# Windowed attention into a softplus MLP: scores of the first three blocks as 64x64 fp32 matmuls, v products of the first two in 64 columns

## The chip, the cores and the metric

The kernel runs on one core of a Trainium2 chip. The metric is the device time of one execution in microseconds (us), taken as the median of several runs. A core has five engines that run side by side, each through its own queue in order: TensorE (PE, matmuls, with the weight loads shown apart as PEld), VectorE (DVE), ScalarE (ACT), GpSimd (POOL) and SyncE (SP), which here issues all DMAs.

## The reference

Eight batches of 576 tokens, eight heads of 64. Each token attends to itself and the 63 tokens before it; the result goes through a two-layer MLP with softplus between.

```python
batch, n_heads, seq, head_dim = (8, 8, 576, 64)
window = 64
scores = scale * np.matmul(q, k.transpose(0, 1, 3, 2))
mask = (rel >= 0) & (rel < window)
scores = np.where(mask, scores, -1000000000.0)
attn = np.exp(scores - np.max(scores, axis=-1, keepdims=True))
attn = attn / (np.sum(attn, axis=-1, keepdims=True) + 1e-09)
...                                  # x: 4608 tokens x 512
h = x @ w_in                         # 512 x 2048
g = np.maximum(h, 0.0) + np.log1p(np.exp(-np.abs(h)))
return (g @ w_out).astype(np.float32)   # 2048 x 512
```

The inputs are fp32 except the two weights, which come in float64 and are handed over as 64-bit words.

## The kernel before

The 4608 tokens are cut into 12 blocks of `TB` = 384. For each block the attention is done in four head pairs (`hp`), each of two heads that together fill 128 partitions; a pair yields 128 rows of the transposed x, kept as two fp32r parts (`x0_*`, `x1_*`). The MLP of a block is 16 steps f: `ffn_up` makes 128 rows of h in 12 matmuls (L405; four pairs by three products of the parts), ACT and DVE form softplus (L409 to L416: `u`, then two fp32r parts `g`), and `ffn_down` adds 9 matmuls (L426) into three PSUM banks. `ffn_up` has two PSUM buffers (`ps_h`), which the DVE's L413 frees.

The passes over f are: block 0 for f 0 to 7, block 1 for all 16, block 0 for f 8 to 15, and then one block after another. Before a step can run, its 1 MB of weights must be loaded and made fp32 from the words (`load_w`: ACT L170, DVE L171 to L174, ACT L177, POOL L178). For f 0 to 11 one set of instructions handles both weights (128x1024, tiles `raws` and `ws`); for f 12 to 15 there are two sets of half the width (128x512, `raw` and `wh`).

Attention comes in two forms. Blocks 0 and 1 (`by_pe`; the first two of `ORDER`, tokens from 0 and from 1152, each at the start of a batch; block 2 holds the tokens from 384) do it in plain fp32: one matmul of 384 columns for each tile of 128 queries gives both heads' scores, because k lies in a block-diagonal tile `kbd` with zeros in the other head's rows (L258). DVE's L269 scales the 192 key columns of a tile and head, adds the mask, keeps the minimum of the negated scores; L275 folds the last 64 columns onto the first 64; ACT takes exp (L279), DVE divides (L284 to L287), the PE transposes (L294), and the product with v takes 12 matmuls, each with a 128-column weight tile `v_pad` in which the other head's columns are zero (L351). All other blocks split q, k into fp32r parts on ACT and DVE (L240 to L247), use 12 matmuls for the scores of a pair (L262), transpose the probabilities by DMA (L311, L316) and multiply bf16 parts of p and v (L380).

The order is set in two ways. Stages of attention, weight conversions and MLP steps are events with a place on one axis (`BASE`, `PACE`, `STG`, `CONVERT`), and are written out in that order. Up to place 100 (some 50 steps) a scheduler that knows estimated durations then orders the instructions of each engine; from there on the PE's order is as written. Once built, every queue is fixed, and at run time each engine waits at its next instruction.

Of the kernel before, what the change touches and what calls it, by code (L numbers as in the profile page):

```python
# [8 lines left out]
F32 = mybir.dt.float32  # L9
BF16 = mybir.dt.bfloat16  # L10
# [21 lines left out]
PE_ORDERED_FROM = 100  # L32
MANUAL = {mybir.EngineType.PE}
# [5 lines left out]
def window_attention_softplus_ffn(  # L39
# [24 lines left out]
    nc = tc.nc  # L64
# [43 lines left out]
    W = CH + P  # L108
# [13 lines left out]
    v_pads = [att.tile([P, 2, NJ, 2, P], F32, name="v_pad", tag=n) for n in ("nat", "tr")]  # L122
    for t in v_pads:
        nc.vector.memset(t, 0.0)
# [4 lines left out]
    mask = cpool.tile([P, W], BF16, name="mask")  # L129
    nc.gpsimd.memset(mask, 0.0)  # L130
    nc.gpsimd.affine_select(
        out=mask, in_=mask, pattern=[[1, W]], compare_op=ALU.is_gt, fill=FAR, base=0, channel_multiplier=-1
    )
    nc.gpsimd.affine_select(
        out=mask, in_=mask, pattern=[[-1, W]], compare_op=ALU.is_ge, fill=FAR, base=CH, channel_multiplier=1
    )

    mask_c = cpool.tile([P, W], BF16, name="mask_c")
    nc.gpsimd.tensor_copy(mask_c, mask)
    nc.gpsimd.memset(mask_c[:, 0:CH], FAR)  # L140
# [43 lines left out]
    def attention(g, hp):  # L184
# [3 lines left out]
        by_pe = g < 2  # L188
# [11 lines left out]
        if by_pe:  # L200
            qf = ld.tile([P, 2, TB], F32, name="q_in") if hp % 2 else ld.tile([P, 2, W - P + TB], F32, name="k_in")
            qf = qf[:, 0, 0:TB]
            kf = kbd_s[hp % 2]
            skip = CH if t0 == 0 else 0
            nc.sync.dma_start(qf, qT[c0 : c0 + P, t0 : t0 + TB])
            for hh in range(2):
                nc.sync.dma_start(kf[heads[hh], hh, skip:], kT[c0 + hh * D : c0 + (hh + 1) * D, t0 - CH + skip : t0 + TB])
        else:
            q_in = ld.tile([P, 2, TB], F32, name="q_in")
            k_in = ld.tile([P, 2, W - P + TB], F32, name="k_in")  # L210
            ts, ks = slice(t0, t0 + TB), slice(t0 - CH, t0 + TB)
# [38 lines left out]
        st = att.tile([P, 2, NJ, W], F32, name="st", bufs=2)  # L250
        mn = att.tile([P, 2, NJ], F32, name="mn", bufs=2)
        sm = att.tile([P, 2 * NJ], F32, name="sm", bufs=2)
        for j in range(NJ):
            sp = bank()
            spv = sp[:, : 2 * W].rearrange("p (h c) -> p h c", h=2)
            js, kc = slice(j * P, (j + 1) * P), slice(j * P, j * P + W)
            if by_pe:
                mm(spv, qf[:, js], kf[:, :, kc], start=True, stop=True)  # L258
# [136 lines left out]
    part = {}  # L395
# [131 lines left out]
```

## Time and profile before

| | |
|---|---|
| median of 3 runs (lowest, highest) | 1041.5 us (1039.78, 1042.13) |
| span of the profiled execution | 1042.4 us |
| PE busy over the span | 990.4 us |
| DVE, ACT, POOL busy | 812.8, 740.3, 56.0 us |
| mean granted TensorE clock | 0.975 |

The profiled execution has no other time of its own than its span, which lies 0.9 us above the median of the runs. In the profile a matmul in plain fp32 is two records (L258, L351), one in fp32r or bf16 is one. A row of a group gives the line, the engine, the operation, output and input tiles, the shape and count, then busy us and mean ns of one, then idle time of the engine just before and what ended it. A row of stretches gives for each engine the busy us and the number of instructions in the stretch.

### The profile page before, as it was taken

The page shows a single profiled execution, that of the slowest core. Times are in us where ns is not written, and L with a number is a line of the kernel's source. Part 1 is how long each engine was busy: PE and PEld are TensorE (multiplying, and loading weights), DVE is VectorE, ACT ScalarE, POOL GpSimd, SP SyncE. Part 2 cuts the span into 40 slices and gives each one's busy share as a digit, 9 for nine tenths or more (in the row PEclk, how much of TensorE's full clock was granted, in tenths as well). Part 3 has the DMA queues.
Part 4 walks back from the last instruction along what each step waited for, and adds up shares of the span by engine and source line. Part 5 has one row for each costly group of instructions (what it writes and reads, how often), then busy time and mean ns, then how long its engine had stood idle before and what let it go on. Part 6 is the DMA issues. An engine that isn't in the chain of part 4 may idle for free.

```text
span 1042.4 us, 16725 instructions
## 1 busy us (share of the span) xinstructions
PE 990.4 (95%) x5888; PEld 879.7 (84%) x5888; DVE 812.8 (78%) x1797; ACT 740.3 (71%) x1705; POOL 56.0 (5%) x54
## 2 busy tenths in 40 slices
PE   5879589999989999999999999999999999999998
PEld 3667478888778889989989989989989998998997
DVE  6889989776977687987987987987987987875322
ACT  4575569777867677877877877877877877875443
POOL 3223520000000000000000000000000000000000
PEclk9889869999999999999999999999999999999999
DMA  6585246435463345744544544543543654731000
GB/s 200 142 274 176 85 146 159 99 97 126 128 146 82 89 104 99 148 108 97 146 113 99 146 111 96 145 114 93 148 115 87 154 114 90 148 53 31 31 1 31
DMA packets 209748, 119.06 MB, mean 114 GB/s; under 512 B 143360, under 2 KB 201728, under 8 KB 208128
## 3 DMA queue, kind: packets, MB, share of 16 engines
q1 hardware_dynamic: 209664, 118.00, 45.7%
q8 instruction: 46, 0.75, 0.3%
q14 instruction: 38, 0.31, 0.1%
HBM read 76.28 MB, written 10.22 MB: 83 GB/s over the span
## 4 chain that ended last, share of the span: by engine, by line
PE 71%; DVE 2%; DMA 1%; ACT 1%; issue 0%; SPq 0%; ACTq 0%; DVEq 0%
PE ps_h L405 31%; PE ps_o L426 31%; PE ps_a L380 4%; PE ps_a L262 4%; DMA tr<-nat 1%; DMA v_in<-in_v_dram 0%; DVE st L269 0%; DVE v L332 0%; DVE raw L443 0%; DVE u L413 0%; DVE nat L314 0%; DVE k L247 0%; ACT nat L310 0%; DVE g L416 0%; DVE xf L386 0%
## 5 line engine op out<-in xcount | busy, mean ns | idle before, releaser
L405 PE MATMUL ps_h<-x,w 128*128 128x384 f32 x2304 | 449.1, 342 | 9.4 <-DVE u L413 7.5
L426 PE MATMUL ps_o<-w,g 128*128 128x512 f32 x1728 | 435.0, 395 | 2.3 <-ACT g L415 2.1
L405 PEld LDWEIGHTS ps_h<-x,w 128*128 128x128 f32 x2304 | 407.1, 190 | 25.4 <-DVE u L413 10.1
L426 PEld LDWEIGHTS ps_o<-w,g 128*128 128x128 f32 x1728 | 317.8, 188 | 61.4 <-ACT g L415 3.0
L409 ACT ACTIVATE u<-ps_h 128x384 f32<-128x384 f32 x192 | 94.0, 489 | 129.5 <-PE ps_h L405 122.8
L413 DVE SCALAR_TENSOR_TENSOR u<-ps_h,u 128x384 f32<-128x384 f32 x192 | 106.3, 554 | 74.4 <-ACT u L411 73.2
L279 ACT ACTIVATE st<-st,mn 128x128 f32<-128x128 f32 x288 | 111.9, 390 | 15.7 <-DVE st L275 15.7
L416 DVE TENSOR_TENSOR g<-u,g 128x384 fp32r<-128x384 f32 x192 | 106.9, 558 | 11.9 <-ACT g L415 9.4
L269 DVE CUSTOM_DVE_ANT_0 st<-ps_a,mask 128x192 f32<-128x192 f32 x216 | 69.7, 352 | 49.4 <-PE ps_a L262 45.8
L410 ACT ACTIVATE u<-u 128x384 f32<-128x384 f32 x192 | 100.6, 525 | 3.3
L411 ACT ACTIVATE u<-u 128x384 f32<-128x384 f32 x192 | 100.3, 522 | 3.8
L262 PE MATMUL ps_a<-k,q_hl 128*128 128x192 f32 x480 | 77.3, 285 | 0.0
L380 PEld LDWEIGHTS <-v 128*128 128x128 bf16 x1088 | 56.1, 98 | 23.9 <-issue 22.1
L380 PE MATMUL ps_a<-tr,v 128*128 128x128 bf16 (+1 forms) x1088 | 70.1, 213 | 3.4 <-DMA tr<-nat 3.4
L415 ACT CAST g<-u 128x384 fp32r<-128x384 f32 x112 | 57.0, 509 | 21.9 <-DVE u L413 21.1
L262 PEld LDWEIGHTS ps_a<-k,q_hl 128*128 128x128 f32 x480 | 67.6, 195 | 3.4
L310 ACT CAST nat<-st 128x768 bf16<-128x768 f32 x40 | 33.2, 830 | 38.4 <-DVE st L308 38.3
L279 ACT ACTIVATION_READ_ACCUMULATOR st<-st,mn 128x1 f32 x288 | 54.0, 187 | 0.0
L385 ACT COPY xf<-ps_a 64x384 f32<-64x384 f32 x80 | 38.1, 477 | 21.2 <-PE ps_a L380 20.1
L287 DVE TENSOR_TENSOR st<-st,sm 128x768 f32<-128x768 f32 x48 | 50.0, 1041 | 1.2
L386 DVE TENSOR_TENSOR xf<-ps_a,xf 64x384 f32<-64x384 f32 x80 | 43.8, 548 | 5.8 <-ACT xf L385 4.6
L329 DVE TENSOR_TENSOR v_in<-v_in,v 128x896 f32<-128x896 f32 x40 | 43.5, 1087 | 4.3 <-ACT v L328 4.3
(82 smaller groups left out, 899.4 us busy)
## 6 DMA issues: line engine op xcount, KB each, us to landing
k_in<-in_kT_dram SPq DMA_DIRECT2D x80, 224.0 KB, 3.8
v_in<-in_v_dram SPq DMA_DIRECT2D x80, 224.0 KB, 3.7
q_in<-in_qT_dram SPq DMA_DIRECT2D x84, 192.0 KB, 4.1
raws<-in_w_words_dram SPq DMA_DIRECT2D x12, 1024.0 KB, 6.0
out_dram<-raw SPq DMA_DIRECT2D x12, 512.0 KB, 2.8
raw<-in_w_words_dram SPq DMA_DIRECT2D x8, 512.0 KB, 5.2
out_dram<-raw SPq DMA_DIRECT2D x12, 256.0 KB, 2.6
v_pad<-in_v_dram SPq DMA_DIRECT2D x52, 32.0 KB, 2.4
```

The lines of the kernel that those rows point to most:

```text
L262: mm(spv[:, hh, :], q_hl[:, hh, js], part[:, hh, kc], start=(hh == 0 and i == 0), stop=(hh == 1 and i == 1), skip_group_check=True,)
L269: nc.vector.tensor_tensor_reduce(st[:, hh, j, :], spv[:, hh, :], m, QSCALE, 3.0e38, ALU.add, ALU.min, mn[:, hh, j : j + 1])
L279: nc.scalar.activation(sv[:, i, 0:P], sv[:, i, 0:P], AF.Exp, bias=mn[:, hh, j : j + 1], scale=-1.0, accum_out=sm[:, i : i + 1])
L380: mm(av[:, osl], (v13 if s else v12)[:, c, hh, :, :], src, start=(i == 0), stop=(i == len(passes) - 1), skip_group_check=True,)
L405: mm(hv, weight(0, a, f)[:, c * P : (c + 1) * P], x[b][c], start=(i_mm == 0), stop=(i_mm == 3 * NC - 1))
L409: nc.scalar.activation(u, hv, AF.Abs)
L410: nc.scalar.activation(u, u, AF.Exp, scale=-1.0)
L411: nc.scalar.activation(u, u, AF.Ln, bias=1.0)
L413: nc.vector.scalar_tensor_tensor(gf, hv, 0.0, u, ALU.max, ALU.add)
L415: (nc.scalar.copy if g < 2 or f % 2 else nc.vector.tensor_copy)(gt[0], gf)
L416: nc.vector.tensor_tensor(gt[1], gf, gt[0].bitcast(F32), ALU.subtract)
L426: mm(ops[g][j], gt[a][:, js], weight(1, b, f), start=(first and i == 0), stop=(last and i == 2),)
```

## The change

For blocks 0, 1 and 2 (`quad`) the scores become 12 matmuls a pair, each of 64 contraction rows (one head), 64 queries and 128 keys; four of them, two heads by two halves of a query tile, use different quarters of the PE array. Each row of scores then holds 128 key columns, not 192: the reduction reads 128 columns and the fold (L275) is gone for these blocks. q and k stay as loaded (`q_two`, `k_two`, both with a half for even and a half for odd pairs), so block 2 has no fp32r split any more. Block 2's probabilities lie otherwise, and its product with v takes 40 matmuls a pair in place of 28. Blocks 0 and 1 hold v without zeros (`v_first`) and multiply 64 weight columns at a time, 12 matmuls a pair as before. New masks of 128 columns are made on POOL; the big memsets of `kbd` and `v_pad` go.

```diff
-    kbd_s = [att.tile([P, 2, CH + TB], F32, name="kbd", tag=f"k{i}") for i in range(2)]
...
+    q_two = ld.tile([P, 2, TB], F32, name="q_two", tag="q_in")
+    k_two = ld.tile([P, 2, CH + TB], F32, name="k_two", tag="k_in")
+    nc.gpsimd.memset(k_two[:, :, 0:CH], 0.0)
...
-    v_pads = [att.tile([P, 2, NJ, 2, P], F32, name="v_pad", tag=n) for n in ("nat", "tr")]
-    for t in v_pads:
-        nc.vector.memset(t, 0.0)
+    v_first = [att.tile([P, 2, NJ, P], F32, name="v_first", tag=n) for n in ("nat", "tr")]
+    for t in v_first:
+        nc.vector.memset(t[0:CH, 0, 0, :], 0.0)
...
+    mask_q = att.tile([P, 3, P], BF16, name="mask_q", tag="k0")
...
-        by_pe = g < 2
+        by_pe = g < BY_PE        # 2
+        quad = g < QUADS         # 3
...
-            nc.sync.dma_start(qf, qT[c0 : c0 + P, t0 : t0 + TB])
-            for hh in range(2):
-                nc.sync.dma_start(kf[heads[hh], hh, skip:], kT[c0 + hh * D : c0 + (hh + 1) * D, t0 - CH + skip : t0 + TB])
+            nc.sync.dma_start(qf, qT[c0 : c0 + P, ts])
+            nc.sync.dma_start(kf[:, skip:], kT[c0 : c0 + P, t0 - CH + skip : t0 + TB])
...
-                for j in range(j0, NJ):
-                    dst = v_pad[rows, lay, j, :, :].rearrange("p h (i d) -> p (h i) d", i=2)[:, 0:4:3, :]
-                    s = start + j * P
-                    nc.sync.dma_start(dst, v[s : s + n, c0 : c0 + P].rearrange("p (h d) -> p h d", h=2))
+                rows_of_v = v[start + j0 * P : start + NJ * P, c0 : c0 + P]
+                nc.sync.dma_start(vf[rows, lay, j0:, :], rows_of_v.rearrange("(j p) n -> p j n", p=P)[0:n])
...
+        if quad:
+            sp = [bank()[:, :TB].rearrange("p (j c) -> p j c", j=NJ) for hh in range(2)]
+            for j in range(NJ):
+                for b, half in enumerate(heads):
+                    for hh, rows in enumerate(heads):
+                        at = j * P + b * CH
+                        mm(
+                            sp[hh][half, j, :], qf[rows, at : at + CH], kf[rows, at : at + P],
+                            start=(j == 0), stop=(j == NJ - 1), skip_group_check=True,
+                        )
+            for j in range(NJ):
+                for hh in range(2):
+                    scaled_min(hh, j, sp[hh][:, j, :])
+                yield
...
-            if by_pe:
-                mm(spv, qf[:, js], kf[:, :, kc], start=True, stop=True)
...
-        nc.vector.tensor_tensor(sv[:, :, 0:CH], sv[:, :, 0:CH], sv[:, :, P:], ALU.min)
+        if not quad:
+            nc.vector.tensor_tensor(sv[:, :, 0:CH], sv[:, :, 0:CH], sv[:, :, P:], ALU.min)
...
-                    mm(
-                        av[:, cs], v_pad[:, a % 2, a // 2, hh, :], pt[:, hh, cs],
-                        start=(hh == 0 and a == 0), stop=(hh == 1 and a == 2 * NJ - 1), skip_group_check=True,
-                    )
+                        for h2, cols in enumerate(heads):
+                            mm(
+                                av[cols, cs], vf[:, a % 2, a // 2, cols], pt[:, h2, cs],
+                                start=(a == 0), stop=(a == 2 * NJ - 1), skip_group_check=True,
+                            )
...
+                        for f in (1, 0):
+                            a = c - f
+                            if 0 <= a < 2 * NJ:
+                                at = ((s * 2 + hh) * 2 * NJ + a // 2 * 2 + f) * P + a % 2 * CH
+                                if f == 1 and c % 2 == 0 and c < NCH - 1:
+                                    passes.append((s, c, trf[:, at : at + P], slice(a * CH, a * CH + P)))
+                                    break
+                                passes.append((s, c, trf[:, at : at + CH], slice(a * CH, a * CH + CH)))
+                        continue
```

Since the scheduler's estimates change, the order of everything up to place 100 changes too. Names such as `x_3_1` below are the x of pair 3 of block 1; line numbers of the changed kernel run 4 to 30 higher (L258 there is the reduction, L268 the scores, L369 the v products, L435 the up matmuls, L443 the `u` step).

At the end of block 1's attention the DVE's order was (L357 the x of its last pair, L241 the split of block 2's q, L171 to L173 a half weight conversion):

```order
L173 SCALAR_TENSOR_TENSOR wh<-raw,wh 128x512
L174 SCALAR_TENSOR_TENSOR wh<-raw,wh 128x512
L357 TENSOR_TENSOR x_3_1_891<-ps_a,x_3_1_890 128x384
L241 TENSOR_TENSOR q_hl<-q_in,q_hl 64x768
L171 TENSOR_SCALAR wh<-wh 128x512
L172 TENSOR_SCALAR wh<-wh 128x512
L173 SCALAR_TENSOR_TENSOR wh<-raw,wh 128x512
```

Now twelve reductions of two pairs of block 2 follow that x, and then these rows up to the first `u` step (L300 to L303 the division, L175 to L177 a half conversion, L443 the `u` step):

```order
L300 TENSOR_SCALAR sm<-sm 128x6
L301 RECIPROCAL sm<-sm 128x6
L303 TENSOR_TENSOR st<-st,sm 128x6x128
L175 TENSOR_SCALAR wh<-wh 128x512
L176 TENSOR_SCALAR wh<-wh 128x512
L300 TENSOR_SCALAR sm<-sm 128x6
L177 SCALAR_TENSOR_TENSOR wh<-raw,wh 128x512
L301 RECIPROCAL sm<-sm 128x6
L443 SCALAR_TENSOR_TENSOR u<-ps_h,u 128x384
```

So between x_3_1 and the first `u` step of block 1 the DVE has twelve reductions, two row sums, one division and three rows of a half conversion, where before it had four reductions, the q split and five rows of half conversions.

On the PE the same place read before (L351 the last v product, L262 the scores of block 2's first pair, of which there are twelve rows):

```order
L351 MATMUL ps_a<-pt,v_pad 128x64 x12
L405 MATMUL ps_h<-x_3_1_890,w_85 128x384 x2
L405 MATMUL ps_h<-x_3_1_891,w_85 128x384
L405 MATMUL ps_h<-x_3_1_890,w_86 128x384
L405 MATMUL ps_h<-x_3_1_891,w_85 128x384
L405 MATMUL ps_h<-x_3_1_890,w_86 128x384
L262 MATMUL ps_a<-k_1145,q_hl 128x192
```

and reads now:

```order
L268 MATMUL ps_a<-k_two,q_two 64x128 x2
L369 MATMUL ps_a<-pt,v_first 64x64 x11
L268 MATMUL ps_a<-k_two,q_two 64x128 x10
L435 MATMUL ps_h<-x_3_1_880,w_85 128x384 x2
L435 MATMUL ps_h<-x_3_1_881,w_85 128x384
L435 MATMUL ps_h<-x_3_1_880,w_86 128x384
L435 MATMUL ps_h<-x_3_1_881,w_85 128x384
L435 MATMUL ps_h<-x_3_1_880,w_86 128x384
L268 MATMUL ps_a<-k_two,q_two 64x128 x24
```

The scores of three pairs of block 2 stand here, where one pair's stood.

More of the change, by code (lines that the diff above doesn't have):

```diff
@@ L32 @@
 PE_ORDERED_FROM = 100
+BY_PE, QUADS = 2, 3
 MANUAL = {mybir.EngineType.PE}
@@ L136, in window_attention_softplus_ffn @@
     )
-    mask_c = cpool.tile([P, W], BF16, name="mask_c")
-    nc.gpsimd.tensor_copy(mask_c, mask)
-    nc.gpsimd.memset(mask_c[:, 0:CH], FAR)
+    mask_q = att.tile([P, 3, P], BF16, name="mask_q", tag="k0")
+    mask, mask_c, mask_b = [mask_q[:, i, :] for i in range(3)]
+    for m in (mask_c, mask, mask_b):
+        nc.gpsimd.tensor_copy(m[0:CH, :], wide[0:CH, 0:P])
+        nc.gpsimd.tensor_copy(m[CH:P, :], wide[CH:P, CH:W])
+    nc.gpsimd.memset(mask_c[0:CH, 0:CH], FAR)
+    nc.gpsimd.memset(mask_b[CH:P, 0:CH], FAR)
@@ L248, in attention @@
         yield
[L250 removed]
+        width = P if quad else W
+        st = att.tile([P, 2, NJ, W], F32, name="st", bufs=2)[:, :, :, 0:width]
         mn = att.tile([P, 2, NJ], F32, name="mn", bufs=2)
         sm = att.tile([P, 2 * NJ], F32, name="sm", bufs=2)
[L253 to L271 removed]
@@ new lines, in attention @@
+        for j in range(NJ if not quad else 0):
+            spv = bank()[:, : 2 * W].rearrange("p (h c) -> p h c", h=2)
+            js, kc = slice(j * P, (j + 1) * P), slice(j * P, j * P + W)
+            for hh in range(2):
+                for i, part in enumerate((k_hi, k_lo)):
+                    mm(
+                        spv[:, hh, :], q_hl[:, hh, js], part[:, hh, kc],
+                        start=(hh == 0 and i == 0), stop=(hh == 1 and i == 1), skip_group_check=True,
+                    )
+            for hh in range(2):
+                scaled_min(hh, j, spv[:, hh, :])
@@ L348, in attention @@
             if by_pe:
[L349 to L355 removed]
+                if hh == 0:
+                    for a in range(2 * NJ):
+                        cs = slice(a * CH, (a + 1) * CH)
+                        for h2, cols in enumerate(heads):
+                            mm(
+                                av[cols, cs], vf[:, a % 2, a // 2, cols], pt[:, h2, cs],
+                                start=(a == 0), stop=(a == 2 * NJ - 1), skip_group_check=True,
+                            )
+                else:
                     nc.scalar.copy(x_t[0], av[:, :TB])
```

61 lines of the change are left out of this document (24 added, 37 removed).

## The prediction

> **What bounds the kernel now.** I read the page's slices first, then a table of stretches, then the end of the prologue in order of time.
>
> ```profile
> span 1042.4 us, 16725 instructions
> ...
> PE   5879589999989999999999999999999999999998
> ...
> DVE  6889989776977687987987987987987987875322
> ...
> PEclk9889869999999999999999999999999999999999
> ```
>
> The PE is nearly full from the sixth slice on (a slice is 26 us), and shows holes only before. The stretches put numbers to that (per engine: busy us and instructions; then granted clock, DMA share, GB/s):
>
> ```profile
> core 0: us, PE busy (x) PEld busy (x) DVE busy (x) ACT busy (x) POOL busy (x), PEclk, DMA share, GB/s
> 0.00:138.00 138.00, 99.78 (x475) 80.51 (x476) 117.02 (x233) 75.10 (x193) 49.86 (x50) 0.87 0.56 173
> 0.00:20.00 20.00, 9.13 (x17) 4.84 (x18) 12.12 (x35) 7.16 (x18) 8.74 (x24) 1.00 0.65 181
> 20.00:60.00 40.00, 34.79 (x181) 28.60 (x180) 31.43 (x80) 21.70 (x69) 8.28 (x6) 0.83 0.64 194
> 60.00:120.00 60.00, 48.79 (x250) 40.48 (x249) 58.83 (x100) 37.39 (x85) 24.59 (x15) 0.94 0.54 177
> 120.00:146.00 26.00, 11.97 (x49) 11.15 (x50) 20.43 (x38) 14.30 (x35) 10.25 (x8) 0.55 0.44 141
> 146.00:300.00 154.00, 148.79 (x901) 131.65 (x900) 124.66 (x279) 119.48 (x280) 4.15 (x3) 0.98 0.49 121
> 300.00:1042.40 742.40, 736.99 (x4496) 663.00 (x4495) 565.29 (x1271) 540.28 (x1224) 0.00 (x0) 1.00 0.43 101
> ```
>
> Three regimes. Behind 146 us the PE is the limit (148.8 of 154, 737 of 742.4): there only PE work counts. From 60 to 120 us the DVE is the limit (58.8 of 60). From 120 to 146 the PE does 12 us in 26. So the time is: when block 1's attention is done and the PE runs full, plus the PE work left. The hinge in order of time, PE and DVE:
>
> ```profile
> 130.35 1.51 PE L294 MATMUL ps_a<-ident,st 128*128 128x128 f32 x6 [10.77 <-DVE st L287]
> ...
> 145.66 1.65 PE L405 MATMUL ps_h<-x,w 128*128 128x384 f32 x4 [3.11 <-DVE u L413]
> ...
> 137.73 0.56 DVE L357 TENSOR_TENSOR x<-ps_a,x 128x384 fp32r<-128x384 f32 x1 [0.41 <-ACT x L356]
> ...
> 145.05 0.55 DVE L413 SCALAR_TENSOR_TENSOR u<-ps_h,u 128x384 f32<-128x384 f32 x1
> ```
>
> The PE waits 10.8 us for the DVE's division of the last pair of block 1 (L287); x_3_1 ends at T = 138.3 us (137.73 + 0.56); then the PE waits again until the first `u` step frees `ps_h`, and runs full from 145.66, that is T + 7.4.
>
> **Term 1: DVE work ahead of T.** The rows of the first 140 us, and the two products that I need later:
>
> ```profile
> L275 DVE TENSOR_TENSOR st<-st 128x384 f32<-128x384 f32 x8 | 5.5, 681 | 0.0
> L269 DVE CUSTOM_DVE_ANT_0 st<-ps_a,mask 128x192 f32<-128x192 f32 x24 | 7.6, 352 | 3.4 <-PE ps_a L258 3.4
> L247 DVE TENSOR_TENSOR k<-k_in,k 128x896 fp32r<-128x896 f32 x1 | 1.6, 1640 | 0.0
> L171 DVE TENSOR_SCALAR wh<-wh 128x512 f32<-128x512 f32 x5 | 3.4, 680 | 2.6 <-ACT wh L170 2.6
> L172 DVE TENSOR_SCALAR wh<-wh 128x512 uint32<-128x512 uint32 x5 | 4.1, 822 | 0.1
> L173 DVE SCALAR_TENSOR_TENSOR wh<-raw,wh 128x512 uint32<-128x512 uint32 x5 | 5.5, 1095 | 0.1
> L174 DVE SCALAR_TENSOR_TENSOR wh<-raw,wh 128x512 uint32<-128x512 uint32 x5 | 4.2, 845 | 0.1
> ```
>
> I counted the DVE's queue up to x_3_1 in both programs. It is the same list but for this: 8 folds go (8 x 0.681 = 5.4 us); 48 reductions shrink from 192 to 128 columns; one split of block 2's k goes (1.6 us); four half conversions stand ahead of x_3_1, not five (0.68 + 0.82 + 1.10 + 0.85 = 3.4 us, which comes back behind T, where the DVE has 30 us to spare in 154). No row shows a reduction of 128 columns: it saves between nothing and a third of 0.352 = 0.117 us; I take the middle, 0.059, since an instruction has a fixed part: 48 x 0.059 = 2.8 us. The memsets of `v_pad` go too, but the DVE stood idle there, waiting for the first scores. Sum 13.2 us of the 117.0.
>
> If the DVE's idle time ahead of T (21 us) stays, T falls by 13.2 to 125.1. Its bounds: half of what is removed could turn into idle time (-6.6), or the idle time could fall too, by the 10 us or so that the DVE stands between 20 and 60 (8.6) and behind 120 (-23).
>
> A second reckoning, because the new order converts more weights early. x_3_0, which lets the first MLP step finish, ends now at 55.2:
>
> ```profile
> 54.61 0.56 DVE L357 TENSOR_TENSOR x<-ps_o,x 128x384 fp32r<-128x384 f32 x1 [1.51 <-ACT x L356]
> ...
> 40.38 2.89 PE L351 MATMUL ps_a<-pt,v_pad 128*128 128x64 f32 x24 [0.29 <-ACT pt L295]
> ...
> L405 PE MATMUL ps_h<-x,w 128*128 128x384 f32 x2304 | 449.1, 342 | 9.4 <-DVE u L413 7.5
> L426 PE MATMUL ps_o<-w,g 128*128 128x512 f32 x1728 | 435.0, 395 | 2.3 <-ACT g L415 2.1
> L258 PE MATMUL ps_a<-kbd,k_in 128*128 128x384 f32 x24 | 12.6, 655 | 5.0 <-DMA kbd<-in_kT_dram 4.9
> L173 DVE SCALAR_TENSOR_TENSOR ws<-raws,ws 128x1024 uint32<-128x1024 uint32 x12 | 15.5, 1292 | 0.1
> L174 DVE SCALAR_TENSOR_TENSOR ws<-raws,ws 128x1024 uint32<-128x1024 uint32 x12 | 16.9, 1406 | 0.1
> ```
>
> In the new queue some 4.7 more full conversions and two half ones stand ahead of x_3_0. A full one is about 1.3 + 1.4 us for the two rows shown and some 1.5 for the other two steps: about 20 us, with the halves 27. Against that stand 5 folds and 30 reductions less (5.2 us) and the idle time that they fill (the DVE had 16.5 us of it by 60, of which I take 5, since 7.9 lie ahead of the first loads). That puts x_3_0 at about 72. From there to T the PE must do 8 steps at 4.6 us ((449.1 + 435.0) / 192) = 37 us and four pairs' attention. Now a pair's v products are 24 records in 2.89 us. The new scores and v products are 24 records a pair each as well; bounds from that row: 2.89 if each record lasts as long, a quarter, 0.72, if four go at once. I take half, 1.45, for both. Four pairs are some 4 x (1.45 + 1.45 + 0.85 for transposes) = 15 us. So 72 + 52 = 124: the PE would be nearly full here. Both reckonings agree, and neither leaves much below 120.
>
> DMAs: a pair's v comes in 2 or 3 issues instead of 9, k in one instead of two. SP is passed by the loads of weights sooner; no wait of the PE on a DMA remains at T, so I cost this at nothing, and count on the DVE's conversions as cover. POOL's new mask copies are eight small ones beside the first loads: the DVE's queue starts with three conversion rows, which wait for the first weights.
>
> **Term 2: the restart.** Behind x_3_1 the DVE now holds twelve reductions, two row sums, a division and three rows of a half conversion ahead of `u`, and the second sum needs twelve exps on ACT. From ACT's rows up to 146 us:
>
> ```profile
> L279 ACT ACTIVATE st<-st,mn 128x128 f32<-128x128 f32 x48 | 18.6, 390 | 10.0 <-DVE st L275 10.0
> L279 ACT ACTIVATION_READ_ACCUMULATOR st<-st,mn 128x1 f32 x48 | 9.0, 187 | 0.0
> L409 ACT ACTIVATE u<-ps_h 128x384 f32<-128x384 f32 x10 | 4.8, 483 | 3.2 <-PE ps_a L258 2.1 <-PE ps_a L351 0.6 <-PE ps_h L405 0.5
> L410 ACT ACTIVATE u<-u 128x384 f32<-128x384 f32 x10 | 5.1, 523 | 0.1
> L411 ACT ACTIVATE u<-u 128x384 f32<-128x384 f32 x10 | 5.2, 520 | 0.0
> L170 ACT ACTIVATE wh<-raw 128x512 f32<-128x512 f32 x7 | 4.7, 671 | 5.1 <-DMA raw<-in_w_words_dram 4.1 <-POOL w L178 1.0
> ```
>
> 12 x 0.577 + 2 x 0.483 + 2 x 0.523 + 0.520 + 0.671 = 10.1 us, 0.4 until the first reduction, 0.55 for `u`: the PE gets its buffer at about T + 11.5, not T + 7.4: +4.1 us. The second `u` stands behind a further division, a half conversion and block 2's first split, some 5 us, of which the PE's next 18 matmuls cover a part: +2 (0 to 5).
>
> **Term 3: PE work behind that.**
>
> ```profile
> L262 PE MATMUL ps_a<-k,q_hl 128*128 128x192 f32 x96 | 14.7, 277 | 0.0
> L380 PE MATMUL ps_a<-tr,v 128*128 128x128 bf16 (+1 forms) x1088 | 70.1, 213 | 3.4 <-DMA tr<-nat 3.4
> ```
>
> Of block 2's scores three pairs at 14.7 / 8 = 1.84 us stood in the full part (-5.5); now three stand in the hole and one behind it (+1.45, by the bounds 0.72 to 2.89). Its v products gain 12 matmuls a pair, 48 at 70.1 / 1088 = 0.064 us: +3.1. Together -1.0 (-1.7 to +0.5).
>
> A rule against the change: a switch between these matmul shapes could cost. The row of L258 shows no idle time of the PE but for DMA, at changes between plain fp32 and fp32r, so the sum has nothing for it. The new PE queue has 46 changes of shape, 42 of them by T + 3; at one v-product record of 0.12 us (2.89 / 24) each they are 5.5 us of PE time ahead of T, and half a microsecond behind it: by that the sum would be -7.6 where it is -8.1 below. The Trainium skill, TensorEngine Tiling (Array Packing), section Tiling Modes, says that changing the tiling mode drains the TensorE, and that tiles run independently of each other; no run here shows either yet.
>
> **The sum.** -13.2 + 4.1 + 2 - 1.0 = -8.1: span 1034.3. The profiled execution is 0.9 above the median of its runs, so 1033.4; I say 1033.
>
> **The rivals.** *The restart eats the gain* (slower). Place: the twelve reductions and exps ahead of `u` after x_3_1. It decides from where the PE restarts some 10 us later than I reckon, at T + 22 (8.1 + 2.1 behind T + 11.5): for instance if the half conversion ahead of `u` waits for its DMA; ACT waited 4.1 us on that one in the rows above. Then 1044 to 1048. Against it: the new order has the conversions done earlier.
>
> *The PE takes over before T* (the same time). If x_3_0 comes at 78 rather than 72, or the shape changes and 2.89 us records apply to four pairs (+12), T is near 133: -5 + 6 - 1, 1041 to 1042. For it: the PE was busy 99.8 of the first 138 us already. Against it: it drops 24 scores of 384 columns and half of the v products' time there.
>
> *The quarters don't run side by side* (the change doesn't do what it says), but the DVE still limits: terms 1 and 2 stay, half of the 12 us above shows: 1037 to 1039.
>
> *The idle time falls as well*, T near 115: 1020 to 1024.
>
> **How the numbers follow.** About 0.2% (2 us) is what a measurement of this kernel can tell from no change. Chances: my forecast, 5 to 15 us faster, 0.55 (own range 1026 to 1038); quarters in sequence 0.08; idle time falls as well 0.10; PE takes over, no change, 0.13; the restart, slower, 0.14. Faster 0.73, same 0.13, slower 0.14. For 8 in 10 the range takes the good end, 1020, and of the slower case the near part: 1020 to 1045.
>
> **What would show it.** Term 1: x_3_1 at 120 to 130 us, the DVE's busy time ahead of it near 104 (117.0 - 13.2), no rows of the fold for blocks 0 to 2, reductions of 128 columns near 0.29 us. Term 2: the first matmul behind the restart about 11 us after x_3_1, waiting for `u`. Term 3: the last block at the same pace, L380 up by 48 matmuls. 24 records of scores in about 1.5 us say half rate, 0.7 four at once, 2.9 none. The forecast is wrong if x_3_1 isn't earlier, or the hole behind it is over 20 us.

## The result, and the profile after

The changed kernel takes 1028.42 us in the median of 4 runs (1027.8 to 1029.83), beside 1041.82 us for the kernel before (4 runs): a ratio of 0.9869, with a 95% interval of 0.9852 to 0.9886. Its profiled execution has a span of 1026.0 us and a time of 1027.8, so a run takes 1.8 us more than its span shows. By the same 1.8 us, that of before (span 1042.4) belongs to the longest of its four runs (1043.84). So the two profiles differ by 16.4 us and the medians by 13.4: some 3 us of what is taken apart below belong to these two executions.

The page of the changed kernel, head and slices:

```profile
span 1026.0 us, 17028 instructions
...
PE   2668979999999999999999999999999999999998
...
DVE  6999585588987888888888878878878887874332
...
PEclk9999989999999999999999999999999999999999
```

The PE starts emptier than before (2668 in the first slices) and then has no hole as deep. One thing in this page misleads: the clock column reads 1.00 in the first stretches, but the matmuls run at half pace there. The same six transposes, early and late:

```profile
74.01 1.51 PE L310 MATMUL ps_a<-ident,st 128*128 128x128 f32 x6 [1.00 <-DVE st L303]
90.54 0.85 PE L310 MATMUL ps_a<-ident,st 128*128 128x128 f32 x6 [1.16 <-DVE st L303]
```

Records of L435 and L456 that follow each other mostly start 1.86 times as far apart up to 81.5 us as behind it. The kernel before had its full pace from 26.4 us on, with gaps (its column shows 0.83 from 20 to 60 us). The stretches that the prediction used, now of the changed kernel:

```profile
core 0: us, PE busy (x) PEld busy (x) DVE busy (x) ACT busy (x) POOL busy (x), PEclk, DMA share, GB/s
0.00:20.00 20.00, 3.11 (x48) 2.37 (x48) 10.75 (x36) 9.99 (x30) 9.65 (x25) 1.00 0.90 324
20.00:60.00 40.00, 25.94 (x176) 19.29 (x176) 40.00 (x75) 20.97 (x54) 16.19 (x11) 1.00 0.65 234
60.00:120.00 60.00, 49.59 (x338) 40.43 (x339) 55.05 (x107) 40.82 (x104) 26.91 (x17) 1.00 0.31 102
120.00:146.00 26.00, 20.88 (x173) 17.63 (x172) 17.19 (x54) 14.65 (x44) 2.11 (x1) 0.87 0.49 146
146.00:300.00 154.00, 150.52 (x978) 132.20 (x977) 116.16 (x258) 115.85 (x260) 4.02 (x3) 1.00 0.48 112
300.00:1026.00 726.00, 721.47 (x4421) 649.13 (x4419) 556.92 (x1254) 532.66 (x1208) 0.00 (x0) 1.00 0.42 102
```

Between 20 and 60 us the DVE has not a moment free (31.43 of 40 before), and from 146 us on the PE is nearly full in both (150.52 of 154 us, 148.79 before). In order of time, the rows of the x tiles (the first is x_3_0, the second x_3_1) and of the restart, PE and DVE:

```profile
70.81 0.51 DVE L375 TENSOR_TENSOR x<-ps_o,x 128x384 fp32r<-128x384 f32 x1
...
128.35 0.56 DVE L375 TENSOR_TENSOR x<-ps_a,x 128x384 fp32r<-128x384 f32 x1 [1.29 <-ACT x L374]
...
136.02 1.69 PE L268 MATMUL ps_a<-k_two,q_two 64*64 64x128 f32 x24 [5.01 <-DMA k_two<-in_kT_dram]
136.89 0.52 DVE L443 SCALAR_TENSOR_TENSOR u<-ps_h,u 128x384 f32<-128x384 f32 x1
137.64 3.17 PE L435 MATMUL ps_h<-x,w 128*128 128x384 f32 x12
```

x_3_0 ends at 71.3 us, x_3_1 at T = 128.9 (138.3 before), and the PE takes up the steps at 137.64, that is T + 8.7 (T + 7.4 before, by the row at 145.66). The scores of block 2's third pair stand in the PE's queue ahead of that restart. They waited 5.01 us for a load of `k_two`, and the steps followed when the scores had been issued.

To see where the 16.4 us of span come from I set the start of every step's matmuls beside the same one of the kernel before (192 steps, counted in the order in which they run; step 32 is block 2's first). Steps 12, 15 and 36 start 8.4, 8.6 and 9.1 us earlier, from step 39 on it is 17 to 20, and from step 51 to the end 16.7. So there are two gains: T, 9.4 us, and some 7.5 us between steps 36 and 51. Between T and step 36 the sum is near nothing (0.3 us lost), made of parts that cancel; they are taken up under terms 2 and 3. The second one is at 280 to 310 us, where the kernel before had a hole. Its PE there, and the stretch of both kernels, before first:

```profile
292.53 0.84 PE L380 MATMUL ps_a<-tr,v 128*128 128x64 bf16 x14 [2.87 <-DMA tr<-nat]
293.20 3.89 PE L405 MATMUL ps_h<-x,w 128*128 128x384 f32 x12
...
280.00:310.00 30.00, 24.47 (x151) 21.27 (x150) 25.52 (x62) 22.18 (x56) 0.00 (x0) 0.94 0.54 119
```

```profile
280.00:310.00 30.00, 29.80 (x175) 26.08 (x174) 23.68 (x54) 22.84 (x58) 0.00 (x0) 1.00 0.55 129
```

Before, the PE waited there for block 3's transposed probabilities (2.87 us on one load of `tr`) and then ran twelve matmuls in 3.89 us where they take 2.24 to 2.38 at full pace; the granted clock is 0.94 over this stretch. In the changed kernel it is busy 29.80 of 30.

### The profile page after: what moved, and what is told of

Read it like the earlier page. It is cut to its first block, busy times and chain, and to the rows that moved or that the text cites. A ratio compares the mean times of both kernels' runs of the same rounds, so it can differ in the third digit from the quotient of the medians.

```text
span 1026.0 us, 17028 instructions
## 1 busy us (share of the span) xinstructions
PE 971.5 (95%) x6128; PEld 861.0 (84%) x6128; DVE 796.1 (78%) x1777; ACT 734.9 (72%) x1697; POOL 58.9 (6%) x55
## 4 chain that ended last, share of the span: by engine, by line
PE 84%; DVE 10%; DMA 3%; issue 2%; ACT 1%; SPq 0%; ACTq 0%; DVEq 0%
PE ps_h L435 37%; PE ps_o L456 37%; PE ps_a L410 5%; PE ps_a L281 5%; DVE ws L177 1%; DVE ws L178 1%; DVE st L258 1%; DVE ws L176 1%; DVE st L303 1%; DVE ws L175 1%; DMA raws<-in_w_words_dram 1%; DMA tr<-nat 1%; DVE u L443 1%; DMA raw<-in_w_words_dram 0%; PE ps_a L268 0%
## 5 line engine op out<-in xcount | busy, mean ns | idle before, releaser
L435 PE MATMUL ps_h<-x,w 128*128 128x384 f32 x2304 | 448.5, 342 | 15.3 <-DVE x L375 9.1
L456 PE MATMUL ps_o<-w,g 128*128 128x512 f32 x1728 | 434.5, 394 | 0.5 <-DVE g L446 0.5
L435 PEld LDWEIGHTS ps_h<-x,w 128*128 128x128 f32 x2304 | 405.6, 190 | 31.0 <-DVE x L375 10.8
L456 PEld LDWEIGHTS ps_o<-w,g 128*128 128x128 f32 x1728 | 318.2, 188 | 58.8 <-DVE g L446 1.3
L439 ACT ACTIVATE u<-ps_h 128x384 f32<-128x384 f32 x192 | 94.0, 490 | 129.2 <-PE ps_h L435 126.5
L443 DVE SCALAR_TENSOR_TENSOR u<-ps_h,u 128x384 f32<-128x384 f32 x192 | 106.2, 553 | 75.6 <-ACT u L441 74.3
L446 DVE TENSOR_TENSOR g<-u,g 128x384 fp32r<-128x384 f32 x192 | 109.1, 568 | 13.0 <-ACT g L445 11.1
L258 DVE CUSTOM_DVE_ANT_0 st<-ps_a,wide 128x192 f32<-128x192 f32 x176 | 57.0, 351 | 44.5 <-PE ps_a L281 44.4
L410 PEld LDWEIGHTS <-v 128*128 128x128 bf16 x1136 | 56.5, 98 | 21.6 <-issue 20.3
L410 PE MATMUL ps_a<-tr,v 128*128 128x128 bf16 (+1 forms) x1136 | 70.2, 211 | 0.2 <-DMA tr<-nat 0.2
L281 PE MATMUL ps_a<-k,q_hl 128*128 128x192 f32 x432 | 69.1, 281 | 0.0
L281 PEld LDWEIGHTS ps_a<-k,q_hl 128*128 128x128 f32 x432 | 59.8, 191 | 3.1
L303 DVE TENSOR_TENSOR st<-st,sm 128x768 f32<-128x768 f32 x48 | 50.2, 1045 | 1.2
L348 DVE TENSOR_TENSOR v<-v_in,v 64x896 bf16<-64x896 f32 x40 | 43.6, 1089 | 5.1 <-PE ps_a L410 2.1
```

The lines of the kernel that those rows point to most:

```text
L258: nc.vector.tensor_tensor_reduce(st[:, hh, j, :], scores, m, QSCALE, 3.0e38, ALU.add, ALU.min, mn[:, hh, j : j + 1])
L281: mm(spv[:, hh, :], q_hl[:, hh, js], part[:, hh, kc], start=(hh == 0 and i == 0), stop=(hh == 1 and i == 1), skip_group_check=True,)
L303: nc.vector.tensor_tensor(pn, pn, sm.unsqueeze(2).to_broadcast([P, 2 * NJ, P]), ALU.mult)
L410: mm(av[:, osl], (v13 if s else v12)[:, c, hh, :, :], src, start=(i == 0), stop=(i == len(passes) - 1), skip_group_check=True,)
L435: mm(hv, weight(0, a, f)[:, c * P : (c + 1) * P], x[b][c], start=(i_mm == 0), stop=(i_mm == 3 * NC - 1))
L439: nc.scalar.activation(u, hv, AF.Abs)
```

## The experiments

Twelve variants ran. Times are medians, of 4 runs where no number is given; ratios are to the kernel before on the same chip. x_3_0 and x_3_1 are from the profiled execution of each.

| run | us | ratio, 95% interval | x_3_0 | x_3_1 |
|---|---|---|---|---|
| before | 1041.8 | 1 | 55.2 | 138.3 |
| changed | 1028.4 | 0.9869 (0.9852 to 0.9886) | 71.3 | 128.9 |
| e1 block 2 old | 1031.5 | 0.9907 (0.9884 to 0.9930) | 72.1 | 129.1 |
| e2 block 2 alone (6 runs) | 1032.8 | 0.9927 (0.9905 to 0.9949) | 50.6 | 132.4 |
| e3 fold added (10 runs) | 1042.0 | 1.0014 (1.0002 to 1.0026) | 80.9 | 141.3 |
| e4 all quarters | 1015.6 | 0.9760 (0.9739 to 0.9781) | 71.6 | 129.2 |
| e5 PE order from 11 | 1023.0 | 0.9821 (0.9800 to 0.9843) | 72.2 | 124.0 |
| e6 same quarter | 1031.3 | 0.9903 (0.9879 to 0.9927) | 68.5 | 129.9 |
| e7 no POOL | 1016.1 | 0.9756 (0.9735 to 0.9777) | 62.0 | 110.8 |
| e8 no division | 1010.5 | 0.9700 (0.9671 to 0.9728) | 50.9 | 102.1 |
| e9 halves late (5 runs) | 1034.0 | 0.9929 (0.9903 to 0.9955) | 70.6 | 124.2 |
| e10 quarters and order | 1006.4 | 0.9665 (0.9643 to 0.9686) | 71.8 | 123.7 |
| e11 all three | 1005.4 | 0.9658 (0.9632 to 0.9683) | 70.4 | 119.5 |
| e12 v products old | 1026.9 | 0.9860 (0.9843 to 0.9876) | 73.4 | 126.7 |

Every edit lets the scheduler plan the first 100 places anew, so each also moves rows that it does not name, and none changes one thing alone; where that decides the reading, it is said.

**e1 and e2: what is the second gain?**

```diff
-BY_PE, QUADS = 2, 3
+BY_PE, QUADS = 2, 2                      # e1
```

```diff
-        by_pe = g < 2                    # e2, in the kernel before
+        by_pe = g < 2
+        quad = g == 2                    # and the quad branches of the change
```

> Block 2 goes back to the old form (split q and k, 192-column reductions, fold, 28 v products a pair); blocks 0 and 1 keep the quarters and the 64-column v products. Two things were gained in the changed kernel: about 9.5 us by the first full step of block 1 (x_3_1 at 128.9 us, not 138.3), and about 8 us more at steps 36 to 39 of the up matmuls (some 285 to 305 us), where the kernel before stood waiting for block 3's attention. Theory A: the second gain comes from block 2 alone, whose splits, folds and wider reductions kept DVE and ACT behind; then the stall returns at steps 36 to 39, block 2's scores cost the PE 1 to 2 us more, and the time is 1035 to 1039. Rival B: the second gain is a debt of the prologue (weight conversions left over from it), which the new blocks 0 and 1 pay early; then no stall, and 1028 to 1031. Both expect x_3_1 at 127 to 132 us.

> The kernel before with block 2 alone in the new form (quarters, reductions of 128 columns, no split, no fold, 40 v products a pair); blocks 0 and 1 as before. Theory A (the loss at 285 to 305 us comes from block 2's own DVE and ACT work): x_3_1 stays at 136 to 139 us, the loss at steps 36 to 39 goes, and the time is 1031 to 1035. Rival B (it is a debt of the prologue): the loss stays, and the time is 1038 to 1042. In both the restart behind x_3_1 may move by some us, since twelve reductions and exps of block 2 take the place of its splits.

e2 did as theory A said, but for T: steps 36 and 39 start 3.9 and 13.6 us earlier than before, so the loss there is gone with block 2 alone in the new form (1032.8, in A's range). x_3_1 came at 132.4, not 136 to 139; of the 5.9 us, block 2's k split is 1.6, and one half conversion fewer stands ahead of x_3_1 (16 rows on `wh`, not 20; that of before at 135 us took 2.2); how the rest came I did not settle. e1 missed A's time (1031.5, and not 1035 or more; it lies just above B's 1031) and place: against the changed kernel it gains 5.1 us by step 12 and loses 10.1 between steps 24 and 27, and ends 4.2 later. Its loss is another wait, on the PE of e1:

```profile
222.55 2.93 PE L456 MATMUL ps_o<-w,g 128*128 128x512 f32 x6 [5.54 <-ACT raw L475]
```

The PE waits 5.5 us for ACT to copy out a finished block, so ACT is behind there, and the granted clock is 0.51 from 221 to 228 us. Block 2's old form costs in both, but what waits depends on the order. The two parts of the change are not additive: block 2 alone takes 8.3 us off its chip's 1041.0, blocks 0 and 1 alone 9.6, both together 13.4.

**e3, e8, e9: does the DVE set T?**

```diff
+        if by_pe:                        # e3, where the fold was
+            for _ in range(1):
+                nc.vector.tensor_tensor(sv[:, :, 0:CH], sv[:, :, 0:CH], sv[:, :, 0:CH], ALU.min)
...
+        if not by_pe:                    # e8
             nc.vector.tensor_tensor(pn, pn, sm.unsqueeze(2).to_broadcast([P, 2 * NJ, P]), ALU.mult)
...
-CONVERT = (-104, -98, -93, -88, -6, -3, 0, 3, 6, 8, 11, 13, 16, 18, 21, 24)
+CONVERT = (-104, -98, -93, -88, -6, -3, 0, 3, 18, 20, 22, 24, 26, 28, 30, 32)   # e9
```

> The changed kernel with one more DVE instruction a pair in blocks 0 and 1, a minimum of the first 64 columns with themselves, of the old fold's shape (128x384 elements, 0.68 us in the kernel before): 8 x 0.68 = 5.4 us of DVE work ahead of x_3_1, nothing for the PE. Theory A, the DVE sets the end of the prologue: x_3_1 goes from 128.9 to about 134, and the time to 1033 or 1034. Rival B, the PE sets it by now (it is busy 10.0 us of the 10 from 110 to 130 us): x_3_1 within 1.5 us, 1028 to 1030.

> The changed kernel without the DVE's division of the probabilities in blocks 0 and 1 (L303, 8 instructions, 10.8 us ahead of x_3_1): the row sums are not divided out there. Nothing goes from PE, ACT or DMA. Theory A, the DVE sets x_3_1 alone: x_3_1 comes 9 to 12 us earlier and the time is 1016 to 1020. Rival B, behind 100 us the PE sets it (10.0 us busy of 10 from 110 to 130 us): x_3_1 comes 1 to 5 us earlier, 1023 to 1028.

> The changed kernel with the places of the last eight weight conversions on the axis moved back (f from 8 on: 6 to 24 before, 18 to 32 now). On the DVE the eight half conversions (12.9 us) that stood ahead of x_3_1 then follow it; the 12 full ones stay ahead; nothing is left out. Theory A, the DVE's work ahead of x_3_1 sets the time, wherever that work goes: x_3_1 comes 9 to 16 us earlier, at 113 to 120 us, and since the DVE has some 22 us idle in the 50 behind 150 us, most of that stays: 1014 to 1021. Rival B, the PE sets x_3_1 behind 100 us, or the work moved behind x_3_1 makes the steps of block 1 wait: 1023 to 1030.

All three missed: e3 and e8 on the far side of theory A, e9 above both ranges. e3 moved x_3_1 by 12.4 us for 6.5 us of added folds, e8 by 26.8 for 10.8 us removed, and e9 only by 4.7 for 13.4 us of DVE work less ahead of it. What tells them apart is x_3_0. The stretches up to x_3_0 and from there to x_3_1, of the changed kernel, e8 and e9:

```profile
0.00:71.30 71.30, 35.20 (x260) 26.09 (x260) 62.05 (x128) 36.44 (x96) 33.51 (x39) 1.00 0.68 241
71.30:128.90 57.60, 52.35 (x384) 43.38 (x384) 46.36 (x95) 36.89 (x94) 19.23 (x13) 1.00 0.28 94
```

```profile
0.00:50.90 50.90, 35.46 (x272) 24.42 (x274) 41.23 (x110) 30.59 (x88) 18.05 (x31) 0.87 0.85 304
50.90:102.10 51.20, 41.82 (x307) 33.75 (x304) 50.99 (x93) 35.36 (x91) 30.83 (x18) 0.83 0.38 127
```

```profile
0.00:70.60 70.60, 35.04 (x262) 26.44 (x263) 60.09 (x121) 36.33 (x97) 36.50 (x40) 1.00 0.65 223
70.60:124.20 53.60, 49.61 (x354) 42.69 (x353) 34.90 (x83) 31.96 (x85) 11.02 (x8) 1.00 0.23 77
```

Up to x_3_0 the DVE is the limit (62.05 of 71.30; it idles only before the first loads) and the PE is half empty. x_3_0 follows the DVE's busy time ahead of it: 20.8 us less of it in e8 brought x_3_0 20.4 earlier, 2.0 less in e9 0.7 earlier, 9.0 more in e3 (71.08) 9.6 later. The plan has a large part in that: e8 has 23 conversion rows on `ws` ahead of x_3_0 and not 35, e3 has 39. Behind x_3_0 the PE is the fuller engine in the changed kernel (52.35 of 57.60, with the DVE idle for 11 us) and in e9 (49.61 of 53.60); there, work taken from the DVE is worth little. In e8 it is not so: the conversions that moved behind x_3_0 keep the DVE busy for 50.99 of 51.20 us, and the PE for 41.82. So neither pure theory holds: T is x_3_0, set by the DVE, and then 49 to 61 us in the variants of the changed kernel, in which the fuller engine depends on where the conversions lie.

e9 ended later than the changed kernel all the same (1034.0; its profiled execution is its longest, 1036.5): between steps 30 and 36 it loses 8.8 us against the changed kernel, in the stretch 250 to 300 us (a row of its PE, and the stretch):

```profile
274.73 2.38 PE L435 MATMUL ps_h<-x,w 128*128 128x384 f32 x12 [2.33 <-DVE u L443]
...
250.00:300.00 50.00, 41.75 (x253) 35.83 (x253) 37.25 (x84) 33.40 (x76) 0.00 (x0) 1.00 0.47 113
```

There the PE waits for `u`, and in smaller amounts for `g`, `tr` and block 3's q split, although block 2 has its new form. So block 2's new form is not enough for the second gain. It was lost where DVE and ACT had more left to do behind T, be it block 2's splits (before, e1) or 13 us of conversions (e9). That is what these runs have in common; no run adds work behind T with the order held, and at which step a backlog is paid I can't derive.

**e5: the restart.**

```diff
-PE_ORDERED_FROM = 100
+PE_ORDERED_FROM = 11
```

> The changed kernel, with the PE's order as written from place 11 on and not from 100 (one number). Block 2's scores then stand behind the first steps of block 1, and on the DVE the first u step follows x_3_1 at once: no reductions, exps and conversion rows between them. In the changed kernel the PE restarts 8.7 us after x_3_1 (128.9, then 137.6), waiting for that u. Theory A: those rows are what the restart waits for; the first full step of matmuls behind x_3_1 starts 2 to 4 us after it, and the time falls by 3 to 6 us, to 1022 to 1026. Rival B: the restart waits for something else (the load of k_two that landed at 136.0 us, block 2's scores), or what is moved comes back as a wait later on: 1027 to 1031.

The time and the place are those of theory A. In e5, DVE and PE around x_3_1:

```profile
123.49 0.56 DVE L375 TENSOR_TENSOR x<-ps_a,x 128x384 fp32r<-128x384 f32 x1 [1.51 <-ACT x L374]
123.51 1.21 PE L435 MATMUL ps_h<-x,w 128*128 128x384 f32 x3 [0.57 <-ACT x L374]
124.55 2.21 PE L456 MATMUL ps_o<-w,g 128*128 128x512 f32 x9
126.60 2.27 PE L435 MATMUL ps_h<-x,w 128*128 128x384 f32 x12
```

From x_3_1 (124.0) to the next full step are 2.6 us, not 8.7, the PE doesn't stop on the way, and the time falls by 5.4 us. But e5 does not tell its two theories apart, since it moves both away: the DVE and ACT rows ahead of `u`, and block 2's scores on the PE with their wait for `k_two`. In the changed kernel the two paths ended together: `u` at 137.41 us, the scores behind the load of `k_two` at 137.6, and the steps at 137.64. What the PE waited for between 129 and 267 us in the changed kernel:

```profile
PE ps_a L268 <- DMA k_two<-in_kT_dram: 5.0, 1, 5.0
PE ps_h L435 <- DVE u L443: 3.3, 2, 1.7
```

The profile puts the wait at the restart down to the load (the 3.3 us on `u` are two later waits, at 149 and 155 us). With the rows ahead of `u` alone taken away, the scores would still have held the PE to 137.6. That load was issued at 130.13, behind two loads of weights (512 KB each, from 129.12), and landed at 135.89.

**e6 and e12: what are the PE's narrow matmuls worth?**

```diff
-            for j in range(NJ):          # e6, scores; for the v products h2 goes outside a
-                for b, half in enumerate(heads):
-                    for hh, rows in enumerate(heads):
+            for hh, rows in enumerate(heads):
+                for b, half in enumerate(heads):
+                    for j in range(NJ):
...
-                                av[cols, cs], vf[:, a % 2, a // 2, cols], pt[:, h2, cs],
+                        av[:, cs], v_pad[:, a % 2, a // 2, hh, :], pt[:, hh, cs],   # e12
```

> The changed kernel with the same score and v-product matmuls in another order: matmuls that use the same quarter (scores) or the same column half (v products) follow each other, so that none can run beside its neighbour. In the changed kernel at full clock two records of scores start per 0.10 us and four where the order has four quarters in a row; two records of v products start per 0.05 us. If neighbours in different quarters run side by side, 24 records of scores take some 2.5 us now and 24 of v products 1.25, not 1.2 and 0.7; if they don't, nothing changes. Theory A, the PE sets x_3_1 behind some 100 us: x_3_1 comes 2 to 6 us later, 1030 to 1035. Rival B, the DVE sets it: within 1 us, 1028 to 1029.

> The changed kernel with the v products of blocks 0 and 1 as before: zero-padded tiles of 128 columns (with their memsets and 9 DMAs a pair), 24 records of 0.11 us each at full clock (2.7 us a pair), not 0.85. The scores of the three blocks stay in quarters. One half conversion more stands ahead of x_3_1 on the DVE. x_3_0 is set by the DVE and stays near 71 us; if from there on the PE sets x_3_1, four pairs cost it 4 x 1.8 = 7 us more: x_3_1 at 134 to 138, 1033 to 1037. If the DVE sets x_3_1, it comes 1 to 3 us later, and the time is 1029 to 1032.

In e12 the padded tiles are filled in the old order of rows, so in every second run of 64 queries the keys are exchanged. Scores and v products on the PE at full pace, of the changed kernel, e6 and e12:

```profile
98.08 0.87 PE L268 MATMUL ps_a<-k_two,q_two 64*64 64x128 f32 x12 [0.74 <-ACT pt L311]
98.89 0.92 PE L369 MATMUL ps_a<-pt,v_first 128*64 128x64 f32 x24
```

```profile
113.07 1.14 PE L268 MATMUL ps_a<-k_two,q_two 64*64 64x128 f32 x12
114.14 1.43 PE L369 MATMUL ps_a<-pt,v_first 128*64 128x64 f32 x24
```

```profile
91.15 0.89 PE L272 MATMUL ps_a<-k_two,q_two 64*64 64x128 f32 x24
91.97 2.89 PE L371 MATMUL ps_a<-pt,v_pad 128*128 128x64 f32 x24
```

Neighbours in different quarters do run side by side: put in the same quarter, 24 v records take 1.43 us and not 0.92, and 12 scores 1.14 and not 0.87. Mostly two ran at a time, since the scheduler issues a bank's six first (one head, two column halves), and 24 scores took some 1.6 us; where the order keeps all four together, 24 take 0.89 (e12's row). Yet e6 lost only 2.9 us: the time is in theory A's range, x_3_1, 1.0 later, in B's. x_3_0 came 2.8 us earlier there, by a new plan, and from it to x_3_1 were 61.4 us and not 57.6, which fits slower matmuls on the PE (3.4 us of half clock, 0.97 in this stretch, are in it too). And e12, with 2.89 us for a pair's v products, missed both its forecasts: it was no slower than the changed kernel (1026.9), and x_3_1 came 2.2 earlier. From x_3_0 to x_3_1 its PE spends some 9 us more on v products, a part of it at half pace (granted clock 0.85), and about two steps fewer stand there; they fill the hole behind x_3_1:

```profile
126.70:150.00 23.30, 23.30 (x137) 19.99 (x136) 11.11 (x31) 12.54 (x31) 1.31 (x1) 1.00 0.35 119
```

The changed kernel is busy 14.40 of 21.10 us from 128.9 to 150. So the narrow v products, as the change stands, save PE time that the PE then waits out; e12's new plan is part of that result.

**e7: the long DVE rows.**

```diff
-                nc.gpsimd.tensor_tensor(lo, w[:, m - m0, :], hi.bitcast(F32), ALU.subtract)
+                nc.scalar.copy(lo, w[:, m - m0, :])
```

> The changed kernel with the 32 subtractions that POOL does in the weight conversion (w less its high part, L182) replaced by copies of w on ACT, so the low part of the weights is left out: it holds the wrong numbers, by the same matmuls. POOL then has nothing to do behind 10 us. In the changed kernel 24 DVE instructions ahead of x_3_1 took 20.8 us longer in all than others of their kind, nearly all of them while POOL ran (in the kernel before 20, 16.7 us). Theory A, DVE and POOL hold each other up: the long ones go, DVE's busy time ahead of x_3_1 falls from 108 to 88 or 90, x_3_1 comes 8 to 15 us earlier and the time is 1014 to 1021, less if ACT's 17 us more of copies come in the way. Rival B, the long ones have another cause: no change of their times, x_3_1 within 2 us.

Theory A, with more at x_3_1 (18.1 us) and less of it kept at the end (12.4 us). The same group of the changed kernel and of e7 (least, middle and longest time in ns):

```profile
L176 DVE TENSOR_SCALAR ws<-ws x12: 676/694/1757, 10.2 to 90.3; 128x1024 uint32<-128x1024 uint32 x12
```

```profile
L176 DVE TENSOR_SCALAR ws<-ws x12: 681/694/695, 10.7 to 77.6; 128x1024 uint32<-128x1024 uint32 x12
```

Without POOL's subtractions no row is long any more, and the DVE's busy time ahead of x_3_1 falls from 108.4 to 85.5.

**e4, e10, e11: better versions.**

```diff
-BY_PE, QUADS = 2, 3
+BY_PE, QUADS = 2, 12                     # e4; e10 with e5's edit; e11 with e5's and e9's
```

> The new form of the scores for all 12 blocks. In the changed kernel a pair's split scores of blocks 3 to 11 stand in three pieces of 0.51, 0.51 and 0.42 us, 1.44 us in all; 24 records of quarters in one piece take 0.80 to 1.05 us at full clock; a head's v products take 0.70 us in the new lay-out (20 matmuls) and 0.77 in the old (14). So the PE, which limits from 146 us on, should lose 0.4 to 0.6 us for each of 36 pairs: 14 to 20 us. Theory A: that shows, 1008 to 1016. Rival B: the changes of matmul shape, or scores that take two banks at once and wait for the DVE, eat it: 1024 to 1035.

> Quarters for all 12 blocks together with the PE's order as written from place 11 on. The first took 12.9 us from the changed kernel's 1028.4, PE work of blocks 3 to 11 and so behind 300 us; the second 5.4 us, at the restart of 130 us. If both are what they seem, they add up: 1009 to 1012. If block 2's attention, now later, makes block 3's late again, 1013 to 1018.

> The three together: quarters for all blocks, the PE's order as written from place 11 on, and the last eight conversions placed later. If the DVE's work ahead of x_3_1 sets the time, it is that of quarters and order less 8 to 13 us, 997 to 1003. If the steps of block 1 then wait for conversions and u steps on the DVE: 1006 to 1012.

e4 gained 12.9 us, some 1.3 a block behind 300 us: the right mechanism, a little less than the 14 to 20 reckoned. L410 has 1568 records then, not 1136, in about the same time (70.3 us beside 70.2), since most are 64 columns wide. With the PE order (e10) it comes to 1006.4: 22.0 us off the changed kernel, more than the 18.3 of both apart and below the forecast range of 1009 to 1012; why they add to more I did not settle. The late conversions (e11) add nothing that can be told (1005.4, between its two ranges; the intervals overlap): x_3_1 comes 4.2 earlier, and half of that is given back between steps 18 and 21. e10 and e11 beat both kernels by over 2%.

## Why the prediction was right, and where its steps were off

The forecast was 1033 (1020 to 1045), faster; it came to 1028.4. The direction and the first gain were as argued; the size was 4.6 us short. That it came so near is partly luck. By the profiles, T fell 3.8 us less than forecast, the way from T to step 36 cost 4.8 us less, and a gain of 7.5 us behind it was not forecast.

**Term 1, T: predicted -13.2, measured -9.4.** Items: the folds 5.4 as reckoned; the reductions 0.282 us and not 0.352, 3.4 us saved (2.8 reckoned; 48 x 0.070); the split 1.6; the half conversion 4.3 (3.4). The memsets of `v_pad` (2.7 us, 0.3 in their place) went too, which the prediction put at nothing. What the list lacked is that the rows that both kernels have did not keep their durations: they took some 8 us more, 6.3 of it in the full conversions and 2.2 in `g`, in rows that ran beside POOL. All rows counted, 24 ahead of x_3_1 were longer than others of their kind, by 20.8 us, where before 20 had been, by 16.7, some of these in the rows that went. So the DVE's busy time fell only from 117.3 to 108.4, and its idle time stayed (21.0, 20.5), as the term assumed. That it stayed is chance: before, 14.7 us of it lay ahead of x_3_0 and 6.3 behind, now 9.3 and 11.2, where the PE was the fuller engine.

**The second reckoning** was the better one: x_3_0 at about 72 (71.3), then 37 us of steps (19.2 + 18.0) and 15 of attention (15.3). It left out the PE's idle time there, 5.2 us, and so said 124 for 128.9. Its prices are those of full pace, and up to 81.5 us the PE ran at half: of the 10.1 us from x_3_0 on it was busy for 9.04, which at 1.86 times the pace would be 4.9, so this alone may be worth 4 us of T (an estimate, and not shown, since the DVE was as full there, 9.98 us). The rival that the PE takes over before T was thus half true: it did, from x_3_0 on, but its work was as short as reckoned, so T still fell. The other rivals did not come: the restart was not 10 us later, neighbours do run side by side (two at a time), and the idle time did not fall.

**Term 2, the restart: predicted T + 11.5, measured T + 8.7.** The place was right, the cause only in part. `u` ended at T + 8.5, but the PE came to the steps at T + 8.7 from the scores that had waited for `k_two`; the prediction put waits of the PE on a DMA at nothing, and this one was 5.0 us. That both paths ended within 0.2 us is luck, and no run separates them. For `u` itself the reckoned 11.5 (its terms add up to 11.1) was too long because I added the rows of an exp and of its read-out, 0.390 + 0.187. They overlap. ACT, behind x_3_1:

```profile
129.55 0.39 ACT L295 ACTIVATE st<-st,mn 128x128 f32<-128x128 f32 x1
129.84 0.18 ACT L295 ACTIVATION_READ_ACCUMULATOR st<-st,mn 128x1 f32 x1
129.94 0.38 ACT L295 ACTIVATE st<-st,mn 128x128 f32<-128x128 f32 x1
```

From one exp to the next are 0.39 us, so twelve take 4.7 and not 6.9. The +2 for the second `u` did come: behind the restart, up to step 36, the PE stood idle for 3.4 us (nearly all of it in two waits on `u`), and for 0.9 before.

**Term 3: v products of block 2, predicted +3.1, measured about 0.** L410 has the 48 records more, 1136 in 70.2 us beside 1088 in 70.1: 48 records of 128 columns went and 96 of 64 came. A mean of a group with two forms was the wrong price.

From T to step 36, terms 2 and 3 said +5.1 together; it was +0.3. The restart gave +1.3 and the idle time behind it +2.5. The PE's busy time behind the restart fell by 3.5 us. About 1.2 of that is the granted clock, which no term had: before, the PE restarted at half pace (0.50 until 150.0 us, 4.34 us of work), now only 1.76 us of work fell into such a stretch (until 139.4). The rest, 2.3, is mostly block 2's scores, without the v products' +3.1.

**What was missed: some 7.5 us at 276 to 310 us.** I read 148.8 busy of 154 as full and costed only PE work behind 146 us. The idle 5.2 us and the granted clock of 0.98 in that row were nearly all one hole: from 276 to 310 us the PE stood idle for 5.5 us, waiting for `tr` (3.4) and `g` (2.1), and 3.4 us more had half the clock. Stretches of 30 us would have shown it. The comparison of the span 1042.4 with the median of times was loose too (a span against times, 1.8 us apart); it moved the forecast by a few tenths, since the same 1.8 would have been added at the end.

## What to carry to other kernels

A milestone is set by a chain that changes engines: find which engine limits on each side of its last hand-over (in the changed kernel the DVE up to x_3_0, the PE behind), since work saved on the other side is mostly waited out. Two waits can end together, as `u` and the load of `k_two` did here; an edit that moves both does not say which one counted. Check the pace by the starts of equal matmuls, and don't take it from the clock column alone. Sum durations of back-to-back rows by start to start, and never price a new shape by the mean of a group with several forms. Where a bound engine is "97% busy" over a long stretch, cut the stretch finely before calling it full: the missing 3% may be one wait that the change takes away.

## What the runs showed of the hardware

DVE and POOL held each other up, one instruction at a time. In the changed kernel, DVE and POOL at 74 us:

```profile
74.57 2.95 POOL L182 TENSOR_TENSOR w<-ws,w 128x512 fp32r<-128x512 f32 x2 [2.65 <-ACT w L181]
74.68 1.71 DVE L176 TENSOR_SCALAR ws<-ws 128x1024 uint32<-128x1024 uint32 x1
```

The DVE row took 1.71 us and not 0.69. It began 0.1 us after the first of POOL's two subtractions, which ended at 75.84, and itself ended 0.55 us after that. The Trainium skill, SBUF — State Buffer, section Who interferes with whom, says that a DVE instruction in a two-port mode and a GpSimd one shut each other out for the whole instruction, and that a DVE instruction with two SBUF inputs contends with a GpSimd one that reads SBUF. The trace agrees: rows that read two SBUF tiles, or apply a scalar to one, were long (up to 2.3 us), and those with an input in PSUM were not: reductions took 0.282 us without POOL beside them and 0.278 with it, `u` steps 0.545 and 0.550. Without POOL's subtractions (e7) no DVE row was long. The change paid 4 us of what it saved in such rows; that a denser DVE meets POOL more often is my reading, and no run varied it alone.

A run of narrow matmuls costs a little at its end. At full pace pairs of score records start 0.10 us apart, and the next shape starts 0.20 after the last pair; before, `v_pad`'s records stood 0.11 apart and the next shape 0.11 behind. So it is 0.10 us a run, by estimate some 1.2 us for the twelve runs between x_3_0 and x_3_1. The Trainium skill, TensorEngine Tiling (Array Packing), section Tiling Modes, says that a change of mode drains the TensorE and that tiles work independently: both agree with these numbers and with e6, and the cost is small here beside the 5 us (42 changes at 0.12) that the prediction reckoned as the price ahead of T if each change cost a record.
